# A third tile's mean shared by two engines, two tiles' first blocks scaled from one PSUM bank, and a weight row loaded in two pieces, in an adaptive-layer-norm attention block

## The chip, the cores and the metric

The kernel runs on one core of a Trainium2 chip. The metric is the device time of one execution, in microseconds (us). The kernel before took 95.64 us, the median of three runs (95.59, 95.64 and 95.98). The core has a matrix engine (TensorE, "PE" in the profile, with its weight loads shown as "PEld"), a vector engine (VectorE, "DVE"), a scalar engine (ScalarE, "ACT"), a general engine (GpSimd, "POOL") and a queue that issues transfers (SyncE, "SP"). Each runs its own instructions in order, and they wait for each other by semaphores. PSUM, the memory that TensorE writes, has eight banks.

## The reference

The inputs are x (2 x 256 x 1152), c (2 x 1152), wqkv (1152 x 3456), wo (1152 x 1152) and w_mod (1152 x 6912), all bf16.

```
mod = (silu(c) @ w_mod).reshape(B, 6, 1, D)
shift_a, scale_a, gate_a, shift_m, scale_m, gate_m = [mod[:, i] for i in range(6)]
h = layernorm(x) * (1 + scale_a) + shift_a
q, k, v = split(h @ wqkv)
p = softmax(q @ k^T * D ** -0.5)
return x + gate_a * ((p @ v) @ wo)
```

Only three of the six parts of mod are used: the shift, the scale and the gate of the attention half.

## The kernel before, in words

The 512 rows of x (two batch items of 256 tokens) are four tiles of 128 rows: tiles 0 and 1 belong to item 0, tiles 2 and 3 to item 1. D = 1152 is nine blocks of 128, numbered k = 0 to 8.

*Order.* Every instruction that goes through the recorders `vec`, `sca`, `ten`, `spq` and `gps` is put down in a list for its engine, and `pin` (L98) fixes the order of each list as it was written. So the order in the text is the order on each engine, and all of them show up in the profile as L85, the line of the recorder. PSUM banks are named by their pool: five in `MM`, and one each in `BA`, `BB` and `BC`. A bank that is asked for again has to wait until its last reader is done.

*Loads.* SP issues all weights and x in a fixed order (L167 to L193): tiles 0, 1 and 2 of x, the first part of the scale weights, row block 0 of K's weights (`load_k(0, 1)`), tile 3 of x (`load_x(3)`, L175), row block 1 of K's weights (L176), the second part of the scale weights in two pieces, then the rest of K's rows with the other parts of the scale weights between them, the shift weights and Q. Each load waits for the one that is eight back in this order, whose semaphore lane it takes over.

*Layer norm.* The mean is subtracted first, and the factor 1/std is left for later, since it is a number per token. Tile 0's mean is found on VectorE; the means of tiles 1 and 2 on ScalarE by a copy with an accumulator over the whole row (`act_mean`, L235); tile 3's mean by ScalarE over 640 columns and VectorE over the other 512 (L401 to L407). VectorE then centres the tile (`centre`). TensorE transposes its nine blocks into two banks (`transposes`, L249; four blocks and five), and VectorE or ScalarE copies them to SBUF (`xcT_copy`, L256).

*Scale.* 1 + scale_a has four parts by blocks: PA is blocks 0 and 1, PB is 2 to 4, PC is 5 and 6, PD is 7 and 8. Part PA is opened by a matmul that writes ones into the bank (`scale_open`, L273), so that the 1 needs no addition. Part PB is worked out with four narrow tiles of the matrix engine (`scale_tiles`, L297), transposed by VectorE, and the 1 is added (`scale_turned`, L304). VectorE multiplies each transposed block by its scale: `scaled` from SBUF, `scaled_tp` from PSUM.

*K.* K^T is accumulated over k. Five of its nine column blocks have banks of their own (`accs`, `k_part`, L322); the other four go in pairs for the first two k (`pair_part`), whose sums are copied out to SBUF and held (`park`). For k = 0 and 1 the K matmuls run in pieces: tiles 0 and 1 together, then tile 2, then tile 3, as each gets ready (L394 to L425). From k = 2 on (`k_step`) a matmul covers all 512 tokens. A later transpose (`pT3`, L466) spreads 1/std over the partitions, ahead of `k_step(5)` (L470).

*After that* come Q, the scores, softmax, V, attention times V and the output projection, one behind the other on TensorE. The change doesn't touch them.

Of the kernel before, what the change touches and what calls it, by code (L numbers as in the profile page):

```python
# [7 lines left out]
ACT = mybir.ActivationFunctionType  # L8
ALU = mybir.AluOpType
AX = mybir.AxisListType  # L10
F32 = mybir.dt.float32
BF16 = mybir.dt.bfloat16
# [4 lines left out]
def kernel(  # L17
# [10 lines left out]
    P = 128  # L28
    B, N, D = x.shape
    T = B * N  # L30
    KT = D // P
    TT = T // P
    NQ = N // P
# [5 lines left out]
    NACC = 5  # L39
    NPARK = KT - NACC  # L40
    PA, PB, PC, PD = (0, 2), (2, 5), (5, 7), (7, KT)
    KA = PA[1]
    NR = 32
# [12 lines left out]
    const = ctx.enter_context(tc.tile_pool(name="const", bufs=1))  # L56
    small = ctx.enter_context(tc.tile_pool(name="small", bufs=4))
# [4 lines left out]
    MM, BA, BB, BC = (psum, "mm"), (psum_a, "pa"), (psum_b, "pb"), (psum_c, "pc")  # L62
# [3 lines left out]
    def bank(shape, name, dtype=None, where=None):  # L66
        if where is None:
            where = ring[turn_no[0] % len(ring)]
            turn_no[0] += 1
        return where[0].tile(shape, dtype or F32, tag=where[1], name=name)  # L70
# [21 lines left out]
    vec = _Rec(nc.vector, dve_seq)  # L92
    sca = _Rec(nc.scalar, act_seq)
# [13 lines left out]
    def tok(b):  # L107
        return slice(b * N, (b + 1) * N)

    def one(t):  # L110
        return slice(t * P, (t + 1) * P)
# [22 lines left out]

    c_sb = const.tile([P, B, KT], BF16)
    x_sb = act.tile([P, TT, D], BF16)
    ones_row = const.tile([1, 2 * NR], BF16)
    gps.memset(ones_row, 1.0)
    sca.preload_act_table_set("natural_log_exp_and_others")
    sca.dma_start(out=c_sb, in_=c.rearrange("b (p k) -> p b k", k=KT))  # L140
# [7 lines left out]
    def load_x(t):  # L148
        spq.dma_start(out=x_sb[:, t, :], in_=x_f[t * P : (t + 1) * P, :])
# [7 lines left out]
    def load_k(k0, k1, c0=0, c1=D):  # L157
        spq.dma_start(out=wK[:, k0:k1, c0:c1], in_=wqkv_v[:, k0:k1, D + c0 : D + c1])
# [13 lines left out]
    load_s(PA, 0, 4)  # L172
    load_s(PA, 4, KT)
    load_k(0, 1)
    load_x(3)  # L175
    load_k(1, 2)  # L176
    load_s(PB, 0, 4)
    load_s(PB, 4, KT)
    load_k(2, 3)
# [39 lines left out]
    nmean = const.tile([P, TT], F32)  # L219
    xc = act.tile([P, TT, D], BF16, tag="a1")  # L220
    xcT = act.tile([P, KT, T], BF16, tag="a2")
    ssum3 = small.tile([P, 1], F32, tag="ssum", name="ssum")

    def bn_part(t, st, s):
        vec.bn_stats(out=st[:, s, :], in_=x_sb[:, t, s * CW : (s + 1) * CW])
# [9 lines left out]
    def act_mean(t):  # L235
        sca.activation(out=xc[:, t, :], in_=x_sb[:, t, :], func=ACT.Copy, scale=-1.0 / D,
                       accum_out=nmean[:, t : t + 1])

    def act_var(t):
        sca.activation(out=xc[:, t, :], in_=x_sb[:, t, :], func=ACT.Square, bias=snm[:, t : t + 1],  # L240
# [2 lines left out]
    def centre(t, scalar, op, c0=0, c1=D):  # L243
        vec.tensor_scalar(out=xc[:, t, c0:c1], in0=x_sb[:, t, c0:c1], scalar1=scalar, scalar2=None, op0=op)

    HALF = ((0, 4), (4, KT))
    tps = {}

    def transposes(t, h, where):  # L249
        k0, k1 = HALF[h]  # L250
        tp = bank([P, 5, P], "tp", BF16, where)
        for k in range(k0, k1):
            ten.transpose(tp[:, k - k0, :], xc[:, t, k * P : (k + 1) * P], ident)
        tps[t, h] = tp

    def xcT_copy(t, h, on_dve, skip=0):  # L256
        k0, k1 = HALF[h]
        dst, srct = xcT[:, k0 + skip : k1, one(t)], tps[t, h][:, skip : k1 - k0, :]
        if on_dve:
            vec.tensor_copy(out=dst, in_=srct)  # L260
        else:
            sca.copy(out=dst, in_=srct)

    s1p = const.tile([P, KT, B], F32)
    hTs = act.tile([P, KT, T], BF16, tag="a3")
# [7 lines left out]
    def scale_open(part, where):  # L273
        n = part[1] - part[0]
        psS[part] = bank([P, n, NR], "psS", where=where)
        ten.matmul(psS[part].rearrange("p j r -> p (j r)"), lhsT=junk[0:1, :P], rhs=ones_row[0:1, 0 : n * NR],
                   start=True, stop=False, skip_group_check=True)
# [16 lines left out]
    wS_v = wS.rearrange("p kk (k j c) -> p kk k j c", k=KT, j=4)  # L294
    sT = const.tile([P, KT, 32], F32)

    def scale_tiles(part, where):  # L297
        psS[part] = bank([P, part[1] - part[0], 32], "psS", where=where)
        for kk in range(KT):
            for j in range(4):  # L300
                ten.matmul(psS[part][32 * j : 32 * j + 32], lhsT=sc_rhs(kk), rhs=wS_v[:, kk, part[0] : part[1], j, :],
                           start=(kk == 0), stop=(kk == KT - 1))

    def scale_turned(part):  # L304
        vec.transpose(out=sT[:, part[0] : part[1], :].rearrange("p k c -> p (k c)"),
                      in_=psS[part].rearrange("p k c -> p (k c)"))
        vec.tensor_scalar_add(out=s1p[:, part[0] : part[1], :], in0=sT[:, part[0] : part[1], 0:B], scalar1=1.0)

    def scaled(k, sl, scalar):
        vec.tensor_scalar(out=hTs[:, k, sl], in0=xcT[:, k, sl], scalar1=scalar, scalar2=None, op0=ALU.mult)  # L310

    def scaled_tp(k, t):
        vec.tensor_scalar(out=hTs[:, k, one(t)], in0=tps[t, 0][:, k, :], scalar1=s1p[:, k, t // NQ : t // NQ + 1],
                          scalar2=None, op0=ALU.mult)

    def scaled_b(k, b):
        scaled(k, tok(b), s1p[:, k, b : b + 1])
# [4 lines left out]
    def k_part(k, sl):  # L322
        for f in range(NACC):
            ten.matmul(accs[f][:, sl], lhsT=wk(k, f), rhs=hTs[:, k, sl],
                       start=(k == 0 and sl.start == 0), stop=False, skip_group_check=True)

    def pair(i, b, where):
        return bank([P, 2, N], "psE", where=where), NACC + 2 * i, tok(b)

    def pair_part(pr, k):  # L330
        ps, f0, sl = pr
        for i in range(2):
            ten.matmul(ps[:, i, :], lhsT=wk(k, f0 + i), rhs=hTs[:, k, sl],
                       start=(k == 0 and i == 0), stop=(k == KA - 1), skip_group_check=True)
# [6 lines left out]
    def park(pr, on_dve=False):  # L341
        ps, f0, sl = pr
        evac(on_dve, held[:, f0 - NACC : f0 - NACC + 2, sl], ps)

    def k_step(k, f0=0, f1=NACC):
        for f in range(f0, f1):
            ten.matmul(accs[f], lhsT=wk(k, f), rhs=hTs[:, k, :],
                       start=False, stop=(k == KT - 1), skip_group_check=True)
# [3 lines left out]
    def held_block(i, rows, where=None):  # L352
        if where is not None:
            psK[i] = bank([P, T], "psK", where=where)
        for k in range(*rows):
            ten.matmul(psK[i], lhsT=wk(k, NACC + i), rhs=hTs[:, k, :], start=(k == KA), stop=(k == KT - 1))
# [10 lines left out]
    centre(0, mvs[:, 0, 0:1], ALU.subtract)  # L367
    act_mean(1)
    centre(1, nmean[:, 1:2], ALU.add)
    act_mean(2)  # L370
    gps.tensor_scalar_mul(out=snm[:, 1:3], in0=nmean[:, 1:3], scalar1=float(D) ** -0.5)
    transposes(0, 0, MM)
    transposes(0, 1, MM)
    xcT_copy(0, 0, True)
    xcT_copy(0, 1, False)
    transposes(1, 0, MM)
    transposes(1, 1, MM)
    scale_rows(PA, 0, 4)
    xcT_copy(1, 0, True)
    centre(2, nmean[:, 2:3], ALU.add)  # L380
    xcT_copy(1, 1, False)
    scale_rows(PA, 4, KT, js=[(0, 1), (1, 2)])
    scaled(0, tok(0), psS[PA][:, 0, 0:1])
    vec.tensor_copy(out=s1p[:, PA[0] : PA[1], :], in_=psS[PA][:, :, 0:B])
    transposes(2, 0, BB)
    transposes(2, 1, BC)
    scaled_tp(0, 2)
    scaled_b(1, 0)
    scaled_tp(1, 2)
    xcT_copy(2, 0, True, skip=KA)  # L390
    xcT_copy(2, 1, False)


    accs = [bank([P, T], "acc", where=MM) for _ in range(NACC)]  # L394
    k_part(0, tok(0))
    k_part(0, one(2))
    pr20 = pair(1, 0, BA)
    pair_part(pr20, 0)
    pr10 = pair(0, 0, BC)
    pair_part(pr10, 0)  # L400
    H3, C3 = 5 * P, 4 * P  # L401
    sca.activation(out=xc[:, 3, 0:H3], in_=x_sb[:, 3, 0:H3], func=ACT.Copy, accum_out=ssum3)
    half3 = small.tile([P, 1], F32, tag="half3", name="half3")
    vec.reduce_sum(out=half3, in_=x_sb[:, 3, H3:D], axis=AX.X)
    vec.tensor_scalar(out=nmean[:, 3:4], in0=half3, scalar1=ssum3, scalar2=-1.0 / D, op0=ALU.add, op1=ALU.mult)
    centre(3, nmean[:, 3:4], ALU.add, 0, C3)
    centre(3, nmean[:, 3:4], ALU.add, C3, D)  # L407
    pair_part(pr10, 1)
    k_part(1, tok(0))
    k_part(1, one(2))  # L410
    park(pr10)
    transposes(3, 0, BB)
    pair_part(pr20, 1)
    transposes(3, 1, BC)
    scaled_tp(0, 3)
    scaled_tp(1, 3)
    xcT_copy(3, 0, True, skip=KA)
    park(pr20)
    xcT_copy(3, 1, False)
    st3 = small.tile([P, NCH, 6], F32, tag="stats", name="stats")  # L420
    bn_part(3, st3, 0)
    act_var(1)
    k_part(0, one(3))
    scale_tiles(PB, BB)
    k_part(1, one(3))  # L425
    scale_turned(PB)
    for k in range(*PB):
        for b in range(B):
            scaled_b(k, b)
    bn_part(3, st3, 1)  # L430
    bn_part(3, st3, 2)
    vec.bn_aggr(out=mvs[:, 3, :], in_=st3)
# [30 lines left out]
    scale_part(PC)  # L463
    held_block(0, (4, 5))
    held_block(1, PB, BC)
    pT3 = bank([P, P], "pT3", BF16, BB)  # L466
    ten.transpose(pT3, parts_sq, ident)
    masked = const.tile([P, TT, P], BF16)
    vec.tensor_tensor(out=masked, in0=pT3.unsqueeze(1).to_broadcast([P, TT, P]), in1=mask, op=ALU.mult)
    k_step(5)  # L470
    held_block(0, (5, 6))
    held_block(1, (5, 6))
    k_step(6, 0, 2)
# [274 lines left out]
```

## Time and profile before

| what | value |
|---|---|
| median of three runs | 95.64 us |
| the profiled execution, its own time | 95.63 us |
| span of the profile | 93.9 us |
| TensorE busy | 89.2 us |
| VectorE, ScalarE, GpSimd busy | 69.6, 33.9, 20.8 us |
| read from HBM, written | 19.76 MB, 1.18 MB |
| granted TensorE clock | 1.0 |

The span is what the profiler saw between the first and the last instruction; the execution's own time has 1.7 us around it. A line of the timeline has the start, the time from its first instruction's start to its last one's end, the engine, the line, the operation, what it writes and reads, and how many instructions are put together in it; the idle time of the engine ahead of it stands in brackets with what ended it. Matmuls are pipelined and overlap: a new 128-column one can start while the last is still draining, so the starts tell more than the ends. Busy shares are means over the whole span; what sets the time is read from the chain of waits.

### The profile page before, as it was taken

How to read it: one execution, taken by the hardware profiler on the slowest of the kernel's cores; microseconds unless marked ns; L12 is line 12 of the kernel's file. 1: busy time of each engine (PE TensorE's matmuls, PEld its weight loads, DVE VectorE, ACT ScalarE, POOL GpSimd, SP SyncE). 2: the span in 40 equal slices, each digit the busy share in tenths (PEclk: the TensorE clock that was granted, in tenths of full speed). 3: DMA queues.
4: the chain of work that ended last, by engine and by line, in shares of the span. 5: the costliest groups of instructions: out<-in, count | busy, mean ns of one | idle time of the engine just before them, and what ended most of it. 6: DMA issues, size and time to landing. Idle time of an engine off the chain costs nothing.

```text
span 93.9 us, 1692 instructions
## 1 busy us (share of the span) xinstructions
PE 89.2 (95%) x664; PEld 52.8 (56%) x664; DVE 69.6 (74%) x134; ACT 33.9 (36%) x69; POOL 20.8 (22%) x26
## 2 busy tenths in 40 slices
PE   3999999999999999999999999999999999999970
PEld 1348884545445444444478665656578665665660
DVE  2478789245997977999999899990028587888880
ACT  5188788002643600284220687324246200000010
POOL 5623000800000000000000000008999990002000
PEclk9999999999999999999999999999999999999999
DMA  2999999999999999999999702200000000312212
GB/s 23 345 282 374 372 397 362 369 410 407 407 405 410 414 408 412 402 373 365 381 407 410 296 17 56 63 0 0 0 0 0 0 0 8 125 42 83 114 45 92
DMA packets 17232, 21.31 MB, mean 227 GB/s; under 512 B 2249, under 2 KB 10569, under 8 KB 17225
## 3 DMA queue, kind: packets, MB, share of 16 engines
q1 hardware_dynamic: 16809, 21.17, 62.3%
q8 instruction: 5, 0.08, 0.3%
q10 hardware_dynamic: 416, 0.04, 0.3%
q14 instruction: 2, 0.02, 0.0%
HBM read 19.76 MB, written 1.18 MB: 223 GB/s over the span
## 4 chain that ended last, share of the span: by engine, by line
PE 91%; DVE 4%; issue 1%
PE ps L85 39%; PE psQ L85 19%; PE acc L85 11%; PE psK L85 7%; PE junk_ps L85 5%; PE s_ps L85 4%; PE tp L85 2%; PE psE L85 2%; PE psS L85 2%; DVE o_sb L85 2%; DVE ga L85 2%; PE psH L85 1%; DVE xc L85 1%; DVE junk L85 1%; PE bc_ps L85 0%
## 5 line engine op out<-in xcount | busy, mean ns | idle before, releaser
L85 POOL PARTITION_ALL_REDUCE gate_bc<-gacc x2 | 13.7, 6886 | 44.6 <-DVE gacc L85 44.6
L85 DVE SCALAR_TENSOR_TENSOR gacc<-wG,scT_f,gacc 128x1152 f32<-128x1152 bf16 x16 | 22.4, 1416 | 0.4
L85 PE MATMUL ps<-wV,hT 128*128 128x384 bf16 x108 | 17.7, 326 | 0.0
L85 PE MATMUL psQ<-hT,wQ 128*128 128x512 bf16 x81 | 17.6, 379 | 0.0
L85 PE MATMUL ps<-wO,attnT 128*128 128x384 bf16 (+3 forms) x108 | 17.2, 322 | 0.0
L85 PEld LDWEIGHTS <-attnT 128*128 128x128 bf16 x117 | 11.1, 98 | 6.5
L85 PEld LDWEIGHTS <-hT 128*128 128x128 bf16 x108 | 10.6, 98 | 6.9
L85 PEld LDWEIGHTS <-wK 128*128 128x128 bf16 x109 | 9.5, 97 | 6.9 <-issue 0.2
L85 PEld LDWEIGHTS <-wQ 128*128 128x128 bf16 x81 | 7.9, 98 | 9.6
L85 PE MATMUL acc<-hTs,wK 128*128 128x512 bf16 (+2 forms) x65 | 11.2, 314 | 0.0
L85 DVE TENSOR_TENSOR ga<-ps,gate_bc 128x384 f32<-128x384 f32 (+3 forms) x12 | 6.5, 545 | 3.0 <-PE ps L85 3.0
L85 ACT CAST qkT<-psQ 128x512 bf16<-128x512 f32 x9 | 4.9, 597 | 10.6 <-PE psQ L85 10.6
L85 DVE CAST attnT<-ps 128x512 bf16<-128x512 f32 (+1 forms) x6 | 3.5, 603 | 6.8 <-PE ps L85 6.8
L85 ACT CAST v_sb<-ps 128x384 bf16<-128x384 f32 x12 | 5.5, 476 | 7.9 <-PE ps L85 7.9
L85 PE MATMUL psK<-hTs,wK 128*128 128x512 bf16 x28 | 7.0, 379 | 0.0
L85 DVE TENSOR_TENSOR o_sb<-ga,x_sb 128x384 bf16<-128x384 f32 (+3 forms) x12 | 6.6, 548 | 0.4
L85 ACT CAST o_sb<-ps 128x128 bf16<-128x128 f32 x1 | 0.3, 265 | 17.3 <-PE ps L85 17.3
L85 PE MATMUL junk_ps<-junk 128*128 128x512 bf16 x11 | 4.9, 629 | 1.5 <-DVE junk L85 1.5
L85 DVE TENSOR_TENSOR hT<-hTs,held 128x512 bf16<-128x512 bf16 x9 | 5.8, 688 | 0.4 <-ACT held L85 0.4
L85 DVE BATCH_NORM_STATS2 stats<-x_sb 128x6 f32<-128x384 bf16 x6 | 3.1, 544 | 2.3 <-DMA x_sb<-in_x_dram 2.3
L85 PEld LDWEIGHTS <-junk 128*128 128x128 bf16 (+1 forms) x13 | 1.6, 134 | 5.0 <-issue 3.4
L85 PE MATMUL s_ps<-qkT 128*128 128x256 bf16 x36 | 4.1, 273 | 0.0
(81 smaller groups left out, 84.2 us busy)
## 6 DMA issues: line engine op xcount, KB each, us to landing
wG<-in_w_mod_dram SPq DMA_DIRECT2D x3, 864.0 KB, 12.5
wV<-in_wqkv_dram SPq DMA_DIRECT2D x3, 864.0 KB, 13.4
wO<-in_wo_dram SPq DMA_DIRECT2D x3, 864.0 KB, 9.0
wH<-in_w_mod_dram SPq DMA_DIRECT2D x2, 1152.0 KB, 9.3
wQ<-in_wqkv_dram SPq DMA_DIRECT2D x4, 576.0 KB, 11.7
wK<-in_wqkv_dram SPq DMA_DIRECT2D x7, 288.0 KB, 7.0
wS<-in_w_mod_dram SPq DMA_DIRECT2D x3, 320.0 KB, 6.3
x_sb<-in_x_dram SPq DMA_DIRECT2D x3, 288.0 KB, 3.4
```

Of the source, the lines that this page charges most:

```text
L85: r = fn(*a, **k)
```

## The change

The diff makes four changes and moves some steps to fit.

1. Tile 2's mean is found as tile 3's was: ScalarE sums 640 columns, VectorE 512, VectorE combines them, and centres in two pieces (`shared_mean`, now used for both tiles).
2. For tiles 0 and 1, the transposes of blocks 0 and 1 of both tiles go into one bank (`firsts`), and the other seven blocks of each tile into another, which ScalarE copies out. VectorE scales the first blocks from PSUM, 256 columns at a time. Tile 2's transposes go eight to `BB` and the ninth to `BA`.
3. Row block 1 of K's weights is loaded as two pieces: columns 0 to 639 ahead of tile 3 of x, the rest behind it.
4. The second scale part is opened by a matmul of ones, and the vector addition of 1 goes; the scalings read the transposed scales themselves.

The steps that move: on TensorE the first pair's matmuls come ahead of tile 2's, the k = 1 matmuls of both pairs come behind all of tiles 0 to 2 and ahead of tile 3's transposes, both of tile 3's K steps come ahead of the second scale part, and `k_step(5)` comes ahead of `pT3`.

```diff
     load_k(0, 1)
+    load_k(1, 2, 0, NACC * P)
     load_x(3)
-    load_k(1, 2)
+    load_k(1, 2, NACC * P, D)
...
+    SPLIT, C_FIRST = 5 * P, 4 * P
+
+    def shared_mean(t):
+        half_a = small.tile([P, 1], F32, tag="half_a", name="half_a")
+        half_v = small.tile([P, 1], F32, tag="half_v", name="half_v")
+        sca.activation(out=xc[:, t, 0:SPLIT], in_=x_sb[:, t, 0:SPLIT], func=ACT.Copy, accum_out=half_a)
+        vec.reduce_sum(out=half_v, in_=x_sb[:, t, SPLIT:D], axis=AX.X)
+        vec.tensor_scalar(out=nmean[:, t : t + 1], in0=half_v, scalar1=half_a, scalar2=-1.0 / D,
+                          op0=ALU.add, op1=ALU.mult)
+        for c0, c1 in ((0, C_FIRST), (C_FIRST, D)):
+            centre(t, nmean[:, t : t + 1], ALU.add, c0, c1)
...
+    def transposes_apart(t, where):
+        if not firsts:
+            firsts["tp"] = bank([P, KA, NQ, P], "tp", BF16, MM)
+        rest_tp = bank([P, KT - KA, P], "tp", BF16, where)
+        for k in range(KA):
+            ten.transpose(firsts["tp"][:, k, t, :], xc[:, t, k * P : (k + 1) * P], ident)
+        for k in range(KA, KT):
+            ten.transpose(rest_tp[:, k - KA, :], xc[:, t, k * P : (k + 1) * P], ident)
+        sca.copy(out=xcT[:, KA:KT, one(t)], in_=rest_tp)
...
-    act_mean(2)
+    shared_mean(2)
     gps.tensor_scalar_mul(out=snm[:, 1:3], in0=nmean[:, 1:3], scalar1=float(D) ** -0.5)
-    transposes(0, 0, MM)
-    transposes(0, 1, MM)
-    xcT_copy(0, 0, True)
-    xcT_copy(0, 1, False)
-    transposes(1, 0, MM)
-    transposes(1, 1, MM)
+    transposes_apart(0, MM)
+    transposes_apart(1, BC)
     scale_rows(PA, 0, 4)
-    xcT_copy(1, 0, True)
-    centre(2, nmean[:, 2:3], ALU.add)
-    xcT_copy(1, 1, False)
     scale_rows(PA, 4, KT, js=[(0, 1), (1, 2)])
-    scaled(0, tok(0), psS[PA][:, 0, 0:1])
+    scaled_firsts(0, psS[PA][:, 0, 0:1])
     vec.tensor_copy(out=s1p[:, PA[0] : PA[1], :], in_=psS[PA][:, :, 0:B])
-    transposes(2, 0, BB)
-    transposes(2, 1, BC)
-    scaled_tp(0, 2)
-    scaled_b(1, 0)
-    scaled_tp(1, 2)
-    xcT_copy(2, 0, True, skip=KA)
-    xcT_copy(2, 1, False)
+    scaled_firsts(1, s1p[:, 1, 0:1])
+    tps[2, 0] = bank([P, KT - 1, P], "tp", BF16, BB)
+    tps[2, 1] = bank([P, 1, P], "tp", BF16, BA)
+    for k in range(KT):
+        ten.transpose(tps[2, 0][:, k, :] if k < KT - 1 else tps[2, 1][:, 0, :], xc[:, 2, k * P : (k + 1) * P], ident)
+    for k in range(KA):
+        scaled_tp(k, 2)
+    vec.tensor_copy(out=xcT[:, KA : KT - 1, one(2)], in_=tps[2, 0][:, KA:, :])
+    sca.copy(out=xcT[:, KT - 1, one(2)], in_=tps[2, 1][:, 0, :])
...
     k_part(0, tok(0))
+    pr10 = pair(0, 0, BC)
+    pair_part(pr10, 0)
     k_part(0, one(2))
     pr20 = pair(1, 0, BA)
     pair_part(pr20, 0)
-    pr10 = pair(0, 0, BC)
-    pair_part(pr10, 0)
...
-    pair_part(pr10, 1)
+    shared_mean(3)
     k_part(1, tok(0))
     k_part(1, one(2))
+    pair_part(pr10, 1)
     park(pr10)
+    pair_part(pr20, 1)
     transposes(3, 0, BB)
-    pair_part(pr20, 1)
     transposes(3, 1, BC)
     scaled_tp(0, 3)
     scaled_tp(1, 3)
+    park(pr20)
     xcT_copy(3, 0, True, skip=KA)
-    park(pr20)
     xcT_copy(3, 1, False)
...
-    k_part(0, one(3))
-    scale_tiles(PB, BB)
-    k_part(1, one(3))
+    for k in range(KA):
+        k_part(k, one(3))
+    scale_open(PB, BB)
+    scale_tiles(PB)
     scale_turned(PB)
     for k in range(*PB):
         for b in range(B):
-            scaled_b(k, b)
+            scaled(k, tok(b), sT[:, k, b : b + 1])
...
+    k_step(5)
     pT3 = bank([P, P], "pT3", BF16, BB)
     ten.transpose(pT3, parts_sq, ident)
     masked = const.tile([P, TT, P], BF16)
     vec.tensor_tensor(out=masked, in0=pT3.unsqueeze(1).to_broadcast([P, TT, P]), in1=mask, op=ALU.mult)
-    k_step(5)
```

More of the change, by code (lines that the diff above doesn't have):

```diff
@@ L136 @@
     x_sb = act.tile([P, TT, D], BF16)
-    ones_row = const.tile([1, 2 * NR], BF16)
+    ones_row = const.tile([1, (PB[1] - PB[0]) * NR], BF16)
     gps.memset(ones_row, 1.0)
@@ L221 @@
     xcT = act.tile([P, KT, T], BF16, tag="a2")
-    ssum3 = small.tile([P, 1], F32, tag="ssum", name="ssum")
     def bn_part(t, st, s):
@@ L262, in xcT_copy @@
             sca.copy(out=dst, in_=srct)
+    firsts = {}
+    def transposes_apart(t, where):
[7 more added lines that the diff above has]
+        sca.copy(out=xcT[:, KA:KT, one(t)], in_=rest_tp)
     s1p = const.tile([P, KT, B], F32)
@@ L295, with scale_tiles @@
     sT = const.tile([P, KT, 32], F32)
-    def scale_tiles(part, where):
-        psS[part] = bank([P, part[1] - part[0], 32], "psS", where=where)
+    def scale_tiles(part):
         for kk in range(KT):
@@ L301, in scale_tiles @@
                 ten.matmul(psS[part][32 * j : 32 * j + 32], lhsT=sc_rhs(kk), rhs=wS_v[:, kk, part[0] : part[1], j, :],
-                           start=(kk == 0), stop=(kk == KT - 1))
+                           start=False, stop=(kk == KT - 1), skip_group_check=True)
     def scale_turned(part):
@@ L306, in scale_turned, with scaled_firsts @@
                       in_=psS[part].rearrange("p k c -> p (k c)"))
-        vec.tensor_scalar_add(out=s1p[:, part[0] : part[1], :], in0=sT[:, part[0] : part[1], 0:B], scalar1=1.0)
     def scaled(k, sl, scalar):
         vec.tensor_scalar(out=hTs[:, k, sl], in0=xcT[:, k, sl], scalar1=scalar, scalar2=None, op0=ALU.mult)
+    def scaled_firsts(k, scalar):
+        vec.tensor_scalar(out=hTs[:, k, tok(0)], in0=firsts["tp"][:, k].rearrange("p t c -> p (t c)"), scalar1=scalar,
+                          scalar2=None, op0=ALU.mult)
     def scaled_tp(k, t):
@@ L398 @@
     pair_part(pr20, 0)
-    pr10 = pair(0, 0, BC)
-    pair_part(pr10, 0)
[L401 to L407, printed above, removed]
-    pair_part(pr10, 1)
+    shared_mean(3)
     k_part(1, tok(0))
     k_part(1, one(2))
+    pair_part(pr10, 1)
     park(pr10)
+    pair_part(pr20, 1)
     transposes(3, 0, BB)
-    pair_part(pr20, 1)
     transposes(3, 1, BC)
```

## The prediction, made before the changed kernel was run

> **What bounds the kernel now.** I read the page first: its shares of busy time, then the chain that ended last.
>
> ```profile
> span 93.9 us, 1692 instructions
> PE 89.2 (95%) x664; PEld 52.8 (56%) x664; DVE 69.6 (74%) x134; ACT 33.9 (36%) x69; POOL 20.8 (22%) x26
> PE 91%; DVE 4%; issue 1%
> ```
>
> TensorE is the path; VectorE enters it at the start and the end only. So the question is when TensorE's unbroken stretch begins. The chain in order of time:
>
> ```profile
> 6.54 0.96 PE tp L85 x13
> ...
> 7.87 0.52 DVE xc L85
> 8.39 0.05 issue
> 8.44 0.68 PE tp L85 x9
> 9.11 0.83 PE acc L85 x10
> ```
>
> The third tile's centring (7.87, on VectorE) releases its nine transposes, and K's first matmuls follow. Next, busy time by stretch, cut at the first K matmul, at 14.17 (the first full-width K step, k=2) and at the last output matmul:
>
> ```profile
> 8.95:14.17 5.22, 5.22 (x95) 4.56 (x92) 4.37 (x17) 4.19 (x7) 0.00 (x0) 1.00 1.07 384
> 14.17:88.19 74.02, 74.02 (x492) 42.36 (x490) 57.34 (x99) 24.22 (x54) 16.53 (x10) 1.00 0.60 223
> ```
>
> The first pair of numbers is length and TensorE's busy time: from 14.17 on it has no gap, and the granted clock is 1.00. Everything changed lies before that but one swap, so the change of time is how far the k=2 step moves from 14.17. The first stretch is less dense than it looks, because a matmul's modelled end covers small gaps; the timeline's starts show them:
>
> ```profile
> 9.66 0.67 DVE L85 TENSOR_REDUCE half<-x_sb 128x1 f32<-128x512 bf16 x1
> 9.74 0.74 ACT L85 ACTIVATE xc<-x_sb 128x640 bf16<-128x640 bf16 x1
> 10.63 0.58 ACT L85 COPY held<-psE 128x512 f32<-128x512 f32 x1
> 10.85 0.65 DVE L85 TENSOR_SCALAR xc<-x_sb,nmean 128x512 bf16<-128x512 bf16 x2
> 11.35 0.38 PE L85 MATMUL tp<-ident,xc 128*128 128x128 bf16 x4
> 11.77 0.47 DVE L85 TENSOR_SCALAR hTs<-tp,s1p 128x128 bf16<-128x128 bf16 x2 [0.27 <-PE tp L85]
> 12.11 0.44 PE L85 MATMUL acc<-hTs,wK 128*128 128x128 bf16 x5
> 12.50 0.57 PE L85 MATMUL psS<-wS,scT_rep 128*32 128x96 bf16 x36
> 13.44 0.16 DVE L85 TENSOR_SCALAR s1p<-sT 128x6 f32<-128x6 f32 x1
> ```
>
> A second chain runs here through tile 3: ScalarE's half mean (9.74), centring (10.85), transposes (11.35), scaling (11.77), tile 3's K matmuls (12.11). Each starts right behind the last, so this chain, not tile 2's, sets 12.11. The landings (issue start plus the landing time of single-load answers) are 8.36 for K's row 0 (3.56 + 4.8), 9.32 for tile 3 of x (4.12 + 5.2) and 10.16 for K's row 1 (4.66 + 5.5):
>
> ```profile
> x_sb<-in_x_dram SPq DMA_DIRECT2D x1, 288.0 KB, 5.2
> ```
>
> **The start of K, tile 2.** Removed: four copies of tiles 0 and 1 out of PSUM (DVE 0.93 for two, ACT 1.26 for two) and ScalarE's full mean of tile 2 (1.16). Added: the half mean, a VectorE sum, the combining step, centring in two pieces, and two ScalarE copies of seven blocks. Tile 2's x is there at 6.35. ScalarE's half takes from 6.35 what tile 3's takes from 9.74, 0.86 to the combining step (10.60): 7.21. VectorE ends tile 1's centring at 6.57, sums 0.67, 7.24. The combining step 0.21, then 0.35 and 0.38: centred by 7.85 and 8.15 instead of 8.38. TensorE ends the first scale part at about 8.06, so the transposes begin at 8.12 instead of 8.44, a gain of 0.32. Of this, half goes: the ninth transpose goes into bank BA, which holds the first scale part until VectorE has read it twice. Those reads wait for that part's end (8.21): the first block of tiles 0 and 1 from PSUM at 8.25, then the copy of the scales. The first is not in the trace: 0.31 is the same width from SBUF; 0.45 is the 128-wide scaling from PSUM (0.28) plus 128 more at the pace of the sum (0.67 for 512); I take 0.35, the PSUM row plus 128 more at the pace of PSUM copies (0.28 for 256, 0.42 for 512), nearest in operation and memory. Less 0.10 of overlap as at 8.29/8.49, plus 0.16 for the copy and 0.05 of wait, the bank is free at 8.71, and K starts at 8.77 instead of 8.95 (8.73 to 8.87). The fifth K matmul needs the bank of the first blocks, read by 9.1, and is reached at 9.21: nothing.
>
> **K's row 1 in two loads.** SP issues one more load (0.43) and tile 3's x moves behind 160 KB. In the stream 576 KB took 10.16 - 8.36 = 1.80 us, so the first piece costs 0.50, and x lands at 9.82 instead of 9.32; row 1 as a whole stays at 10.16. The queue is 5 us deep, so SP's later issues, each a lane further, stay hidden; were that cover gone, each would cost its 0.4 issue. Bounds: no cost (9.32) to a whole load's step of 0.96 (10.28). I take 9.82 because the stream behaves by bytes. The first piece is needed at 8.77 + 1.26 = 10.03, landed by about 8.9; the second at 10.86. Neither waits.
>
> One rule speaks against the split. The Trainium skill (DMA: Bandwidth & Descriptors, section Measured (HBM→SBUF, 128 partitions, SWDGE, issued from GpSimd)) has 0.95 us for 64 KB and 6.15 for 1 MB, and advises loads of 1 MiB or more; by a line through these an added load would cost an estimated 0.6 us on top of its bytes, and the sum below would be near 96.4. The trace does not agree so far: 288 KB loads land 0.84 to 0.96 apart, where that line gives 2.1.
>
> **Tile 3's chain.** It was ScalarE-bound (its copy ended at 9.84); now ScalarE is free at 9.2 (copies 7.31, 8.10, 9.01 at 0.90, 0.90, 0.27, from 0.69 for five blocks) and waits for x: 9.82 + 0.09 = 9.91, 0.17 later than 9.74. VectorE's six-block copy (0.57, by 0.28 for 256 and 0.42 for 512) ends at 9.99, its sum at 10.58: hidden. The chain's fixed 2.37 (9.74 to 12.11) gives 12.28 for tile 3's matmuls.
> There is a second way to the same point. The pair's k=1 matmuls now run after all of tiles 0 to 2: the second starts at 8.77 + 2.20 = 10.97 (ahead of it fifteen matmuls of 0.109, the pairs' spacing from 9.77 to 10.43, and ten of 0.056, tile 3's between 13.00 and 13.29). Their copy to SBUF, queued on ScalarE, starts 0.31 later (10.32 to 10.63 before), at 11.28, instead of 10.63, takes 0.585, and frees bank BC, into which the last five transposes go: 11.91 with 0.05 of wait, plus 5 x 0.056, 12.19. Behind these waiting transposes stand tile 3's matmuls and all that follows. Before, the copy had ended at 11.21, and the other pair's two matmuls filled TensorE meanwhile. So two waits meet at 12.19 and 12.28; the later sets it, 0.17 after 12.11.
>
> **The second scale part.** It now comes behind both tile 3 steps. From 12.28: ten matmuls, 0.56; opening with the ones, 0.06 (0.02, the step of narrow matmuls, to 0.16, what the opening took in the chain); 36 tiles to their end, 0.57; 0.05 and the transpose, 0.32; no addition of 1 (saves 13.63 - 13.44 = 0.19); two scalings, 0.20 and 0.28, and 0.06 to TensorE: 2.10, against 2.06 before. TensorE's own way, 0.56 + 0.06 + 0.50 + 0.88 for the pairs, would be there 0.10 earlier. The bank for the opening is free at 12.6, before it is asked for. So k=2 starts at 14.38 instead of 14.17.
>
> **The swap at k=5** (the rstd transpose behind it): k=5's scaling ends at 19.15, when TensorE reaches it; nothing, at most 0.05. It hides the 0.25 for which the weight load waited on GpSimd.
>
> **Sum.** +0.21. The profiled execution took 95.63 (span 93.9 plus 1.7 around it), the median is 95.64: 95.84 and 95.85, so 95.8.
>
> **Rivals.**
> - The early start survives: x lands near 9.6, because its last packets are the late ones, and the pair's copy ends earlier. For it: K starts 0.15 earlier for certain work saved. Against: both waits above must shrink. All later work 0.15 earlier: 95.5.
> - Slower: the added load costs a whole step, x lands at 10.28, ScalarE starts at 10.37, tile 3's matmuls 12.74, k=2 at 14.84: +0.67, 96.3. It decides from a landing past 9.75 (the pair's copy is the later wait before that) and is over 0.5% from 10.1. For it: an issue more, and landings whose spacing varies by 0.12. Against: pacing by bytes. The Trainium skill's rule on added loads (DMA: Bandwidth & Descriptors) ends about here.
> - The change does nothing that reaches k=2: 95.6. The bounds of the scaling (0.04 less to 0.10 more), of the opening (0.04 less to 0.10 more) and of the swap make 95.75 to 96.1 of my forecast.
>
> **Chances.** Forecast 0.50, early start 0.18, nothing 0.10, late x 0.17; 0.05 for the unseen. A measurement tells about 0.5% (0.48) from no change. Faster by more would need 0.48, more than the early start has: 0.06. Slower by more: 0.17, most of late x and some unseen. Within: 0.77. The range takes in the early start with 0.1 for unlike runs, 95.4, and late x, 96.3.
>
> **What would show it.** Tile 2's transposes at 8.12 with the ninth held until 8.71; K at 8.77; ScalarE's tile 3 mean waiting for x until 9.9; the last tile 3 transposes waiting for ScalarE's copy; tile 3's matmuls at 12.28; k=2 at 14.38, and no TensorE gap behind it. Wrong if x lands by 9.4 or past 10.1, or if a K or scale load comes late behind 14.

## The result, and the profile after

The changed kernel took 96.10 us (median of 13 runs, 95.86 to 96.63), the kernel before 95.68 in as many runs beside it. The ratio is 1.0048, with a 95% interval of 1.0025 to 1.0071: slower by 0.46 us, 0.24 to 0.68. The forecast was 95.8, slower by 0.2: the direction is right, the size about twice the forecast, and the measured time lies in the range that was given.

The profiled execution of the changed kernel took 96.55, with a span of 94.8; it is one of the five slower of the 13 executions. From its page, busy shares and the engines' part of the chain that ended last:

```profile
span 94.8 us, 1694 instructions
PE 89.7 (95%) x665; PEld 53.0 (56%) x665; DVE 70.6 (74%) x134; ACT 33.7 (36%) x69; POOL 20.9 (22%) x26
PE 91%; DVE 4%; ACT 1%; issue 1%
```

The shares say almost nothing; ScalarE is new in the chain with 1%. Busy time by stretch, cut as in the prediction at the first K matmul, at the k = 2 step and at the last output matmul (the first pair of numbers is the length and TensorE's busy time):

```profile
8.86:14.98 6.12, 5.62 (x94) 4.65 (x95) 4.62 (x16) 4.63 (x10) 0.00 (x0) 1.00 1.07 375
14.98:89.06 74.08, 74.08 (x491) 42.44 (x490) 57.72 (x99) 23.75 (x52) 16.68 (x10) 1.00 0.59 219
```

Before, the first stretch was 5.22 long and now it is 6.12; the second was 74.02 and is 74.08. So nearly all of the loss lies between the first K matmul and k = 2, and TensorE now visibly stands still there for 0.5. The 0.06 behind k = 2 is taken up in the last part, at the swap at k = 5. The chain in order of time shows what it waited for:

```profile
8.31 0.36 DVE hTs L85
8.67 0.08 DVE s1p L85
8.75 0.05 issue
8.79 0.23 PE tp L85
9.02 0.55 PE acc L85 x5
...
11.11 0.23 PE psE L85 x2
11.34 0.02 issue
11.36 0.59 ACT held L85
11.96 0.39 PE tp L85 x4
12.35 0.02 issue
12.37 0.30 DVE hTs L85
12.67 0.04 issue
12.71 0.72 PE acc L85 x10
13.43 0.64 PE psS L85 x37
14.07 0.98 PE psE L85 x8
15.05 3.33 PE acc L85 x15
```

At 8.67 the ninth transpose of tile 2 waits for the copy of the scales. At 11.36 the chain goes over the pair's copy on ScalarE, and at 12.37 over VectorE's scaling of tile 3. From the timeline of the same execution, the lines of tile 3's chain:

```profile
9.42 0.55 DVE L85 COPY xcT<-tp 128x768 bf16<-128x768 bf16 x1
10.34 0.74 ACT L85 ACTIVATE xc<-x_sb 128x640 bf16<-128x640 bf16 x1 [1.01 <-DMA x_sb<-in_x_dram]
10.34 0.69 DVE L85 TENSOR_REDUCE half_v<-x_sb 128x1 f32<-128x512 bf16 x1 [0.37 <-DMA x_sb<-in_x_dram]
11.20 0.21 DVE L85 TENSOR_SCALAR nmean<-half_v,half_a 128x1 f32<-128x1 f32 x1 [0.18 <-ACT xc L85]
11.45 0.65 DVE L85 TENSOR_SCALAR xc<-x_sb,nmean 128x512 bf16<-128x512 bf16 x2
11.92 0.52 PEld L85 LDWEIGHTS <-xc 128*128 128x128 bf16 x9 [0.66 <-issue]
11.95 0.66 PE L85 MATMUL tp<-ident,xc 128*128 128x128 bf16 x9 [0.40 <-ACT held L85]
12.71 0.72 PE L85 MATMUL acc<-hTs,wK 128*128 128x128 bf16 x10
13.36 0.21 PE L85 MATMUL psS<-ones_row,junk 1*128 1x96 bf16 x1
13.50 0.57 PE L85 MATMUL psS<-wS,scT_rep 128*32 128x96 bf16 x36
```

ScalarE and VectorE both stood waiting for tile 3 of x until 10.34, 0.60 later than ScalarE had begun before (9.74). Tile 3's K matmuls start 2.37 behind that, at 12.71, which is the same 2.37 as before the change, and k = 2 starts 2.27 later, where 2.06 was enough before. The pair's copy ends at 11.95, just as tile 3's transposes begin, and so the profile names it as what ended their wait; but the first piece of the centring ends at 11.80 and the first weight load of the transposes is there at 11.92, before the copy's end. So in this execution the centring, and with it x, sets them.

This raised two questions. Is x's late landing the cause, or an accident of this execution? And what do the pairs' new place and the scale part's new place each cost?

### The profile page after: what moved, and what is told of

It is laid out like the page before. It is cut to its first block, busy times and chain, and to the rows that moved or that the text cites. A ratio compares the mean times of both kernels' runs of the same rounds, so it can differ in the third digit from the quotient of the medians.

```text
span 94.8 us, 1694 instructions
## 1 busy us (share of the span) xinstructions
PE 89.7 (95%) x665; PEld 53.0 (56%) x665; DVE 70.6 (74%) x134; ACT 33.7 (36%) x69; POOL 20.9 (22%) x26
## 4 chain that ended last, share of the span: by engine, by line
PE 91%; DVE 4%; ACT 1%; issue 1%
PE ps L85 38%; PE psQ L85 18%; PE acc L85 11%; PE psK L85 6%; PE junk_ps L85 5%; PE s_ps L85 4%; PE psS L85 2%; PE tp L85 2%; PE psE L85 2%; DVE o_sb L85 2%; DVE ga L85 2%; PE psH L85 1%; DVE hTs L85 1%; ACT held L85 1%; DVE junk L85 1%
## 5 line engine op out<-in xcount | busy, mean ns | idle before, releaser
L85 PE MATMUL ps<-pT,v_sb 128*128 128x256 bf16 x36 | 4.1, 272 | 0.0
```

Source lines behind the costliest of these rows:

```text
L85: r = fn(*a, **k)
```

## The experiments

Two theories. A: the first piece of row 1 makes x late, and x alone sets tile 3's chain. B: the pairs' k = 1 matmuls, moved back, make ScalarE's copy of them late, and with it bank BC for tile 3's last five transposes. Beside them the scale part. All ratios below are against the kernel before, run on the same chip in the same job, with 95% intervals; a median of 12 runs carries about 0.2 us either way (experiment 1 has only six runs), so the profiles' rows do much of the telling-apart. A profile is one execution, and not always a typical one. Experiments 9 to 11 ran on another chip than the rest, so they are compared with the others by their ratios.

**1. Row 1 in one load again** (changed kernel otherwise).

```diff
-    load_k(1, 2, 0, NACC * P)
     load_x(3)
-    load_k(1, 2, NACC * P, D)
+    load_k(1, 2)
```

> The changed kernel with K's row 1 in one load behind tile 3 of x, as before the change; all else as changed. Theory A (the split makes x late, and x alone sets tile 3): x is there near 9.4, ScalarE's half mean of tile 3 starts near 9.5 in place of 10.34, and K's k=2 step falls from 14.98 to about 14.2; the time falls by 0.7 to 0.8 against the changed kernel's profiled execution. Theory B (the pair's copy on ScalarE holds bank BC): x is early as well, but the last five transposes wait for the copy until about 12.0, tile 3's matmuls start near 12.3 and k=2 near 14.55: only 0.4 of it comes back, and the kernel stays about 0.35 slower than before the change, 96.0.

Measured: 96.48 beside 95.72, ratio 1.0088 (1.0059 to 1.0118). That is not faster than the changed kernel but, by the ratio, slower than it was (1.0048, 1.0025 to 1.0071; the two intervals overlap a little). From its timeline:

```profile
9.78 0.74 ACT L85 ACTIVATE xc<-x_sb 128x640 bf16<-128x640 bf16 x1 [0.37 <-DMA x_sb<-in_x_dram]
10.56 1.00 PE L85 MATMUL acc<-hTs,wK 128*128 128x256 bf16 x10
11.82 1.07 ACT L85 COPY held<-psE 128x512 f32<-128x512 f32 x2 [1.21 <-PE psE L85]
11.84 0.39 PE L85 MATMUL tp<-ident,xc 128*128 128x128 bf16 x4
12.45 0.44 PE L85 MATMUL tp<-ident,xc 128*128 128x128 bf16 x5 [0.23 <-ACT held L85]
12.73 0.72 PE L85 MATMUL acc<-hTs,wK 128*128 128x128 bf16 x10
```

The half mean starts at 9.78, 0.56 earlier than in the changed kernel, and yet tile 3's matmuls start at 12.73. The last five transposes wait for the pair's copy (12.45), because the k = 1 matmuls began only at 10.56, when row 1 had landed. So theory A falls for this order: x alone doesn't set tile 3's chain. It is not a clean test of an earlier x, because row 1 as one load also puts the k = 1 matmuls back (10.12 in the changed kernel); experiment 5 is that test. B stands, and the split seems to help the order that it was made with.

**2. The split alone** (in the kernel before).

```diff
+    load_k(1, 2, 0, NACC * P)
     load_x(3)
-    load_k(1, 2)
+    load_k(1, 2, NACC * P, D)
```

> The kernel before with K's row 1 in two loads and nothing else. Theory A: x comes 0.5 to 0.95 later, ScalarE's half mean of tile 3 starts near 9.9 to 10.3 in place of 9.74, and every later step moves by 0.15 to 0.6: 95.8 to 96.25. The rival, that the stream paces by bytes and the other parts of the change made the delay: at most 95.8, with tile 3's half mean at 9.9.

Measured: 95.72 beside 95.72, 1.0016 (0.9993 to 1.0038). The half mean started at 9.77, waiting 0.22 for x, against 9.74 before, where ScalarE itself was the late one. The split costs the old order nothing clear of the noise; the interval leaves room for 0.36. Two of the twelve executions took 96.38 and 96.61, longer than any of the 29 of the kernel before (up to 96.16); they have no profile.

**3. One load, and the pairs in their old places.**

```diff
     shared_mean(3)
+    pair_part(pr10, 1)
     k_part(1, tok(0))
     k_part(1, one(2))
-    pair_part(pr10, 1)
     park(pr10)
-    pair_part(pr20, 1)
     transposes(3, 0, BB)
+    pair_part(pr20, 1)
```

> As whole_row, and the first pair's k=1 matmuls stand ahead of tiles 0 to 2's k=1 matmuls again, the second pair's between tile 3's transposes, as before the change. Theory B: the pair's copy is done by 11.2, nothing waits for bank BC, tile 3's matmuls start at 12.05 to 12.15 and k=2 at 14.3: 0.25 less than whole_row, 95.75. Theory A alone: no difference from whole_row.

Measured: 96.03 beside 95.72, 1.0037 (1.0020 to 1.0054); 0.45 less than experiment 1 in the same job, whose interval it doesn't touch; 0.25 less, and 95.75, had been expected. The profiled execution, 95.79, is among the shortest of the twelve: in it the pair's copy ended by 11.13, tile 3's matmuls started at 11.97, and k = 2 started at 14.23. So the pairs' place is worth this much where row 1 is late.

**4. The front alone.** Experiment 3, with the second scale part as before the change.

```diff
-    for k in range(KA):
-        k_part(k, one(3))
-    scale_open(PB, BB)
-    scale_tiles(PB)
+    k_part(0, one(3))
+    scale_tiles(PB, BB)
+    k_part(1, one(3))
...
-            scaled(k, tok(b), sT[:, k, b : b + 1])
+            scaled(k, tok(b), s1p[:, k, b : b + 1])
```

> As whole_row_pairs, and the second scale part is as before the change (its tiles between the two K steps of tile 3, the 1 added on VectorE). What is left is tile 2's shared mean, the first blocks scaled from one bank, and the swap at k=5. If the scale part's new place costs 0.2 (2.27 from tile 3's matmuls to k=2 in the changed kernel, 2.06 before): k=2 near 14.1, 95.55. If moving it costs nothing: as whole_row_pairs. If the early start of tile 2 were worth its 0.1 at K's first matmul all the way: 95.5.

Measured: 95.82 beside 95.72, 1.0011 (0.9992 to 1.0030): 0.21 less than experiment 3, and no different from before; 95.55 had been expected. From tile 3's matmuls to k = 2 it is 2.06 again (12.36 to 14.42 in its profile). But the front's own work earns nothing either; experiment 9 asks why.

**5. x ahead of both pieces** (changed kernel otherwise).

```diff
-    load_k(1, 2, 0, NACC * P)
     load_x(3)
+    load_k(1, 2, 0, NACC * P)
     load_k(1, 2, NACC * P, D)
```

> The changed kernel with tile 3 of x ahead of both pieces of K's row 1; still two pieces, all else as changed. If x behind the first piece is what costs the time: tile 3's half mean starts near 9.5 and the kernel falls from 96.1 to about 95.75. If the pairs' place is what costs it (the second theory): the first piece lands at about 9.9, just before it is asked for, tile 3's last transposes still wait for the copy on ScalarE until about 12, and the time stays at 96.0 to 96.1.

Measured: 96.09 beside 95.78, 1.0048 (1.0023 to 1.0072), the changed kernel's own ratio, as theory B expected. Four of the twelve executions took 96.37 to 96.80, though x comes first here. From its timeline:

```profile
9.09 0.74 ACT L85 ACTIVATE xc<-x_sb 128x640 bf16<-128x640 bf16 x1
10.51 0.21 DVE L85 TENSOR_SCALAR nmean<-half_v,half_a 128x1 f32<-128x1 f32 x1
11.21 1.07 ACT L85 COPY held<-psE 128x512 f32<-128x512 f32 x2 [1.29 <-PE psE L85]
11.26 0.38 PE L85 MATMUL tp<-ident,xc 128*128 128x128 bf16 x4
11.85 0.44 PE L85 MATMUL tp<-ident,xc 128*128 128x128 bf16 x5 [0.20 <-ACT held L85]
12.12 0.72 PE L85 MATMUL acc<-hTs,wK 128*128 128x128 bf16 x10
```

ScalarE begins at 9.09, 1.25 earlier than in the changed kernel's first profile, waiting for nothing. Two other waits take over: the combining step comes at 10.51 behind VectorE's six-block copy and sum, and the last transposes at 11.85 behind the pair's copy.

**6. The scale part alone** (in the kernel before): the reverse of the edit of experiment 4.

> The kernel before with the second scale part's change alone: opened by a matmul of ones, behind both K steps of tile 3, no addition on VectorE. By the prediction's terms (2.10 for 2.06 from tile 3's matmuls to k=2): 0.04 slower, 95.75. By the rows of the changed kernel (2.27, of which the opening has 0.24 where 0.06 was taken): 0.2 slower, 95.92. The rival that the part is worth its saved addition: 0.1 to 0.2 faster, 95.55.

Measured: 95.84 beside 95.78, 1.0008 (0.9988 to 1.0027). The interval holds both 0 and 0.2, so the times don't decide. The rows do:

```profile
12.21 0.72 PE L85 MATMUL acc<-hTs,wK 128*128 128x128 bf16 x10
12.86 0.21 PE L85 MATMUL psS<-ones_row,junk 1*128 1x96 bf16 x1
13.00 0.57 PE L85 MATMUL psS<-wS,scT_rep 128*32 128x96 bf16 x36
13.62 0.28 DVE L85 STREAM_TRANSPOSE sT<-psS 128x96 f32<-128x96 f32 x1 [0.61 <-PE psS L85]
14.47 0.38 PE L85 MATMUL acc<-hTs,wK 128*128 128x512 bf16 x1
```

From tile 3's matmuls to k = 2 it is 2.26, as in the changed kernel, without any other part of the change. By the medians the kernel is only 0.06 slower.

**7. No opening** (changed kernel, the 1 of the second scale part left out, so that blocks 2 to 4 are multiplied by scale_a).

```diff
-    scale_open(PB, BB)
-    scale_tiles(PB)
+    scale_tiles(PB, BB)
```

> The changed kernel without the opening matmul: the 1 of the second scale part is left out altogether, so blocks 2 to 4 are multiplied by scale_a instead of 1 + scale_a. If the opening costs what the rows say: 0.15 to 0.24 less than the changed kernel, 95.85 to 95.95. If it lies beside other work: no difference, 96.1.

Measured: 96.02 beside 95.78, 1.0029 (1.0006 to 1.0051), by the median 0.08 less than the changed kernel and within its interval. In the profile, tile 3's matmuls to k = 2 took 2.13 (12.55 to 14.68) instead of 2.27: the opening is 0.14 of it.

```profile
12.55 0.72 PE L85 MATMUL acc<-hTs,wK 128*128 128x128 bf16 x10
13.20 0.57 PE L85 MATMUL psS<-wS,scT_rep 128*32 128x96 bf16 x36
14.68 0.38 PE L85 MATMUL acc<-hTs,wK 128*128 128x512 bf16 x1
```

This execution's 12.55 is again a wait for the pair's copy, though x was there in time: ScalarE's half mean started at 9.69.

**8. The pairs between** (changed kernel, split kept).

```diff
     k_part(1, tok(0))
+    pair_part(pr10, 1)
     k_part(1, one(2))
-    pair_part(pr10, 1)
     park(pr10)
-    pair_part(pr20, 1)
     transposes(3, 0, BB)
+    pair_part(pr20, 1)
```

> The changed kernel, split kept, with the first pair's k=1 matmuls between tiles 0-1's and tile 2's k=1 matmuls and the second pair's between tile 3's transposes. If the wait for bank BC costs the time: the copy starts 0.28 earlier, tile 3's last transposes no longer wait for it, and the kernel falls by 0.15 to 0.35, 95.75 to 95.95. If x alone sets tile 3: no difference, 96.1.

Measured: 95.99 beside 95.78, 1.0024 (1.0002 to 1.0046): 0.1 less than the changed kernel, in the expected direction, but just short of the expected 95.75 to 95.95 and within the intervals. The last transposes waited for nothing, and tile 3's matmuls started at 12.14, held by VectorE: the combining step came 1.81 behind the first K matmul, as in the front alone.

**9. The six-block copy on ScalarE** (front alone otherwise), behind tile 3's half mean.

```diff
-    vec.tensor_copy(out=xcT[:, KA : KT - 1, one(2)], in_=tps[2, 0][:, KA:, :])
...
     shared_mean(3)
+    sca.copy(out=xcT[:, KA : KT - 1, one(2)], in_=tps[2, 0][:, KA:, :])
```

> front_alone with the copy of tile 2's six blocks moved from VectorE, ahead of tile 3's sum, to ScalarE, behind tile 3's half mean. If that copy is what eats the early start (tile 3's combining step comes 1.81 behind the first K matmul in every run with the copy on VectorE, 1.65 before the change): the step comes at 1.4 to 1.6, tile 3's matmuls 0.1 to 0.2 earlier than in front_alone, and the kernel at 95.6 to 95.7, faster than front_alone's 95.82 and not slower than before. If x alone or TensorE's own queue sets tile 3: no difference, 95.8.

Measured: 95.75 beside 95.74, 1.0010 (0.9988 to 1.0032). The combining step came 1.35 behind the first K matmul (8.99 to 10.34) instead of 1.81 (9.04 to 10.85 in experiment 4, the front alone), and tile 3's matmuls 3.07 behind it instead of 3.32: the copy was the bound there.

```profile
10.85 0.21 DVE L85 TENSOR_SCALAR nmean<-half_v,half_a 128x1 f32<-128x1 f32 x1
```

```profile
10.34 0.21 DVE L85 TENSOR_SCALAR nmean<-half_v,half_a 128x1 f32<-128x1 f32 x1
```

The first is experiment 4, the second this run. The times show nothing of it: the ratio is 1.0010, and experiment 4's was 1.0011.

**10. The pairs between, and the scale part as before.**

> pairs_mid with the second scale part as before the change; K's row 1 split as in the change. If the opening's place costs 0.2 in this surrounding too: 0.2 less than pairs_mid, 95.8, that is about the kernel before. If the scale part is free here: no difference, 96.0.

Measured: 95.95 beside 95.74, 1.0032 (1.0007 to 1.0057), where 95.8 was expected; by the ratio that is no better than experiment 8 (1.0024), which has the new scale part. Its profiled execution took 95.74, with tile 3's matmuls at 12.12 and k = 2 at 14.17, 2.06 apart before rounding, as expected; but five of its twelve runs took over 96.0, as far as 96.45. What held those has no profile.

**11. Everything that the runs pointed to**: tile 2's part, x ahead of both pieces, the pairs between, the copy on ScalarE, and the old scale part (the edits of 4, 5, 8 and 9 together).

> What the runs point to: tile 2's shared mean and the first blocks from one bank, tile 3 of x ahead of both pieces of row 1, the first pair's k=1 matmuls between tiles 0-1's and tile 2's, the six-block copy on ScalarE, the second scale part as before the change. If the three waits found (the pair's copy, the six-block copy, the opening) are all of the loss: k=2 at 13.9 to 14.1, 95.45 to 95.6, faster than before by 0.1 to 0.3. The rival: the second scale part's second piece of weights lands at 12.4 to 12.6, and whatever comes earlier waits for it: 95.65 to 95.75.

Measured: 95.72 beside 95.74, 1.0006 (0.9984 to 1.0028). The loss is gone, and no gain took its place: 95.45 to 95.6 had been expected, and the rival's 95.65 to 95.75 came. The rows don't show the rival's wait for the scale weights, though: the scale tiles (12.68) start 0.09 behind the K matmuls ahead of them. In its profile, of an execution of 95.96, tile 3's last transposes still wait for the pair's copy (12.03, the copy done at 11.98), and K began at 9.17.

**12. The changed kernel again**, unchanged, for a second profile.

> The changed kernel once more, unchanged, for a second profiled execution: in the first, tile 3 of x was there at 10.31, later than in any other run. If that landing is an accident of the execution: x is there at 9.5 to 9.9, tile 3's combining step comes 1.81 behind the first K matmul, tile 3's matmuls start near 12.25 behind the copy on ScalarE, k=2 near 14.5, and this execution takes 96.0 to 96.1. If the late landing belongs to the split: x again past 10.1, k=2 near 14.9, 96.5.

Measured: 96.27 beside 95.83, 1.0039 (1.0018 to 1.0060), an execution of 96.47 profiled:

```profile
9.01 0.72 PE L85 MATMUL acc<-hTs,wK 128*128 128x256 bf16 x5
10.17 0.74 ACT L85 ACTIVATE xc<-x_sb 128x640 bf16<-128x640 bf16 x1 [0.76 <-DMA x_sb<-in_x_dram]
11.04 0.21 DVE L85 TENSOR_SCALAR nmean<-half_v,half_a 128x1 f32<-128x1 f32 x1 [0.18 <-ACT xc L85]
12.55 0.72 PE L85 MATMUL acc<-hTs,wK 128*128 128x128 bf16 x10
```

x was late again, 10.15. But with the same loads, x landed by 9.57 to 9.75 in experiments 2, 7, 8 and 10. So a landing past 10 belongs neither to the split in every execution nor to one execution alone.

**All profiles together.** Tile 3's K matmuls start at the latest of three moments. The first is ScalarE's half mean plus 2.37. The second, where the six-block copy is on VectorE, is the first K matmul plus 3.32 (1.81 to the combining step and 1.51 from there). The third is the end of the pair's copy plus 0.31. From there it is 2.06 to k = 2 with the old scale part, 2.27 with the new one, and 2.13 without the opening.

| kernel | first K | half mean | pair's copy ends | tile 3's K: latest of | seen | k = 2 |
|---|---|---|---|---|---|---|
| changed | 8.86 | 10.34 | 11.95 | 12.71 / 12.18 / 12.26 | 12.71 | 14.98 |
| changed, again | 9.01 | 10.17 | 12.11 | 12.54 / 12.33 / 12.42 | 12.55 | 14.81 |
| x ahead of both | 8.70 | 9.09 | 11.80 | 11.46 / 12.02 / 12.11 | 12.12 | 14.39 |
| no opening | 9.13 | 9.69 | 12.23 | 12.06 / 12.45 / 12.54 | 12.55 | 14.68 |
| pairs between | 8.82 | 9.68 | 11.63 | 12.05 / 12.14 / 11.94 | 12.14 | 14.40 |
| front alone | 9.04 | 9.57 | 11.39 | 11.94 / 12.36 / 11.70 | 12.36 | 14.42 |

Each of the three is the latest in some execution. The next one stands 0.08 to 0.12 behind it in four of the rows, and 0.42 to 0.45 in two. That fits with what the times did when one of them alone was taken away (experiment 5 the first, experiment 8 the third): they moved by 0.1 or less.

## Why the prediction was right, and where its terms were off

*The bound and the place.* Right. TensorE's time from k = 2 on was 74.08, for 74.02 before, and the executions follow k = 2: the time of each minus its k = 2 lies between 81.46 and 81.66.

*Tile 2.* In the changed kernel's first profile, right to 0.1. The transposes began at 8.12 as predicted, the ninth was held by the scale copy until 8.79 (8.71), and K began at 8.86 (8.77). The scaling of the first blocks took 0.356 for the 0.35 taken. But the gain of 0.18 at K's first matmul isn't borne out, and the match of 8.86 can't be told from chance. In the eleven profiles with the new front K starts between 8.65 and 9.17, with a mean of 8.93; in the three with the old one (the kernel before and experiments 2 and 6) at 8.95, 8.68 and 9.04, with a mean of 8.89. What holds the transposes differs: tile 2's centring in some executions, TensorE's own first scale part or the weights for it in others. So that the early start was worth nothing in the end, as forecast, has a simpler reason besides the waits named: over the profiles none can be seen.

*The split.* The sum used 9.82 for x, by bytes. The six executions with a piece ahead of x have it at 10.31, 10.15, 9.75, 9.66, 9.66 and 9.57, a mean of 9.85; the eight with x ahead have 9.76 to 9.07, a mean of 9.32. So the added delay is the 0.50 of the sum, but only as a mean: single executions lie up to 0.5 off. The price of an extra load itself doesn't show in the mean. This bears on the Trainium skill's rule (DMA: Bandwidth & Descriptors, section Measured (HBM→SBUF, 128 partitions, SWDGE, issued from GpSimd)) that was weighed. By a line through that section's figures x would have landed at an estimated 10.4; the mean of 9.85 doesn't agree and lies at the bytes' end.

*Tile 3's chain.* The two waits that were forecast to meet, at 12.19 and 12.28, are both there, in different executions. A third was called hidden and stands right behind them: VectorE's six-block copy is the latest in pairs between and in front alone. It is hidden only where x or the pair's copy is later. Put at the changed kernel's own first K (8.86), its pair's copy and the mean x (9.85, so a half mean at 9.94), the three moments are 12.31, 12.18 and 12.26.

*The second scale part.* This is the term that was sized wrong. The prediction had 2.10 from tile 3's matmuls to k = 2, with 0.06 for the opening; all profiles with the opening behind tile 3 have 2.26 or 2.27. From the last of the ten matmuls the rows have 0.09 to the opening and 0.14 from it to the tiles, 0.24 in all. The opening itself lies within the bounds given, 0.02 to 0.16: 0.14, also by the run without it. What the sum left out is the 0.09 ahead of it, where the form of the matmuls changes; without the opening (experiment 7) the same 0.09 stands between the K matmuls and the scale tiles. The times show this cost less clearly than the rows: 0.21 between experiments 3 and 4, but 0.06 in experiment 6, and nothing between experiments 8 and 10.

With 2.27 in place of 2.10, and from 12.31, k = 2 comes at 14.58, 0.41 later than before; with the 0.06 of the swap below that is 0.47, for 0.46 measured. This is an estimate, put together from one execution's first K and a mean of x. The two executions of the changed kernel that were profiled, 96.55 and 96.47, had x past 10. That is the late-x rival in its landing and nearly in its time (put at 96.3, with a chance of 0.17), but not shown in its cause, as the last paragraph says. Whether the other executions above 96.4 had it too isn't known; experiment 5 has such times with x ahead of both pieces.

*The swap at k = 5.* It was put at nothing, at most 0.05, and costs 0.06: k = 5's first matmul starts 0.28 behind the one before it instead of 0.22, right behind VectorE's scaling. From k = 2 to the first matmul with the shift weights, which stands behind the swap, it is 13.84 in all eleven profiles with the swap and 13.78 in the three without.

*Not settled.* What makes x land past 10 in some executions was not found; in the first profile one of the load's sixteen parts was there at 10.31 and all the others by 9.61. The piece ahead of x and the one behind it show the same in that execution: the last part at 9.59 (the prediction had 8.9) with the others by 8.80, and at 10.62 with the others by 9.95. In the second profile one part is late already in the scale load ahead of K's row 0 (7.90, the others by 7.42), which the change doesn't touch. So the lag runs through several loads, and the traces don't show that the split makes it. And why five of experiment 10's executions took over 96.0, with both known costs taken away, stays open.

## What to carry to other kernels

When an engine runs without a gap from some point on, take the point where the gapless stretch begins and write its start as the latest of all chains that lead to it, with their measured lengths; here the first two of them mostly lay 0.1 us apart, and shortening one brought nothing that could be measured. A matmul that is moved back also moves back the copy that frees its bank, and whoever is queued for that bank: look up the bank's next user before the order is changed. Replacing a small vector addition by a matrix instruction is not free: the addition took 0.19 on VectorE beside other work, and its replacement 0.14 in the one queue that everything waits for, 0.21 together with its new place. And one profile of each kernel can't show a gain of 0.2 where the same step moves by 0.5 between executions.

## What was not expected of the hardware

TensorE runs its first matmuls at half pace, and the moment at which this ends differs from execution to execution, for the same eleven matmuls at the start. In the kernel before and in experiment 2, by the timeline:

```profile
1.50 4.87 PE L85 MATMUL junk_ps<-junk 128*128 128x512 bf16 x11 [1.50 <-DVE junk L85]
```

```profile
1.51 3.88 PE L85 MATMUL junk_ps<-junk 128*128 128x512 bf16 x11 [1.51 <-DVE junk L85]
```

Eleven matmuls end a whole microsecond apart (4.87 or 3.88 long), because in the second the spacing falls from 0.43 to 0.22 after the sixth. Where it is late, the first transposes go at 0.107 instead of 0.056 each, nine steps of them in the profile of experiment 11, where K began at 9.17. The two profiles where it came earliest, of experiments 2 and 3, have the earliest K, 8.68 and 8.65. With the loads' scatter this is probably a part of the spread between executions of one kernel, and a reason to compare rows within one execution rather than single times.
